# Transposes of u, q and k: from TensorE to the DMA crossbar, with three token-mixing tiles of a batch moved ahead

## The chip, the cores and the metric

One NeuronCore of one Trainium2 chip. The metric is the device time of one execution in microseconds (us); lower is better. A program runs as five instruction streams (TensorE, VectorE, ScalarE, GpSimd, SyncE), in the profile PE, DVE, ACT, POOL and SP, and one set of 16 DMA engines that all streams share. Each stream runs its instructions strictly in the order in which they were written.

## The reference

Two stages follow each other. Shapes: batch 4, 8 heads, 768 tokens, head dimension 64, model width 512, hidden width 2048.

```python
# stage 1: attention with 4 sink tokens and a causal window of 128
scores = scale * np.matmul(q, k.transpose(0, 1, 3, 2))
keep = (pos[None, :] < n_sink) | ((rel >= 0) & (rel < window))    # rel = query - key
a = softmax(np.where(keep, scores, -1e9))
x = np.matmul(a, v)            # then laid out as batch, token, 8*64
# stage 2: a residual MLP block
a1 = alpha1 * x + beta1
tok = np.einsum('ts,bsd->btd', w_tok, a1)        # mixes tokens: each tile needs all of a1
u = x + lam * tok
a2 = alpha2 * u + beta2
out = u + lam * (np.maximum(a2 @ w_ch1, 0.0) @ w_ch2)
```

Inputs and output are fp32; the kernel computes in fp16 with fp32 sums.

## The kernel before, in words

Tokens are cut into six tiles of 128 (`NR`), heads into four pairs (`HP`). For each of the four batches there are two halves.

The attention half of a batch: SP loads q and k for each head pair (`load_qk`, eight loads of 384 KB into the eight `nat` buffers) and v (`load_v`, six loads of 256 KB). `trans` casts one loaded tile to fp16 (`n16`, on POOL), TensorE transposes it in six 128x128 matmuls into a PSUM bank (`tp`, L416), and ACT or DVE copies the result to `qkT` (L226 and L228 are the lines of the copy helper). Then come `sinks`, `scores` (S, L499; exponentials on ACT, L514; masks on DVE, L523), and `pv` (L546), whose normalised result is `x`; POOL makes `xh` = alpha1*lam*x + beta1*lam of it (L588, L591).

The MLP half: `tok` (L677) is six matmuls for each of six token tiles, and needs `xh` of all six. DVE adds the result to x (L686), which gives u, and ACT or POOL casts u to fp16 (`u16`). `uTs` transposes u on TensorE, three token tiles (a "chunk") and two of the four column blocks at a time (`uTp`, L712, six matmuls), and ACT (L723) or DVE (L725) applies alpha2 and beta2 while it copies to `uT`. `mlp1` (L738) has 16 groups of four matmuls for each of the two chunks, each group with a relu on ACT (L744) or DVE (L746) into `hT`. `mlp2` (L762) has four quarters of four matmuls for each token tile; DVE adds its result to x (L773) and SP stores the tile.

The attention of batch b+1 is woven into the MLP of batch b. The order is made by a planner while the kernel is built: `add` records a task with a priority, the engines that may do it and their costs, what it waits for and which buffers it uses; `emit` repeatedly picks the task that can start earliest by its own estimate of time, ties going to the lower priority number, and writes it to that engine's stream. The priorities of the MLP of batch b are `STEP*b` plus the place in the list `seq`; the attention steps of batch b+1 are spread between two places of it, `lo` and `hi`. PSUM has four banks of the kind `d` (used by `tp`, `uTp`, `tok`, `h`, `pv`, `ch`) and two pairs of banks for scores. Loads for batch b+2 wait until the fourth mlp2 tile of batch b is done.

The program that is built has eight completion semaphores for its DMAs, given out in rotation in the order in which the DMAs are written; a DMA that takes one up again first waits, on the engine that issues it, for the DMA that had it before.

Of the kernel before, what the change touches and what calls it, by code (L numbers as in the profile page):

```python
# [39 lines left out]
class Plan:  # L40
# [22 lines left out]
    def emit(self):  # L63
        order = sorted(range(len(self.tasks)), key=lambda i: (self.tasks[i].prio, i))
        rank = {id(self.tasks[i]): r for r, i in enumerate(order)}
        waiting = {id(t): len(t.needs) for t in self.tasks}
        open_ = []

        def admit(t):
            bisect.insort(open_, (rank[id(t)], t), key=lambda x: x[0])  # L70

        for t in self.tasks:
            if not waiting[id(t)]:
                admit(t)
        free = {e: 0.0 for e in (PE, ACT, DVE, POOL, SP)}
        mode = None
        channel = 0.0
        port = 0.0
        done = 0
        while done < len(self.tasks):  # L80
            best = None
            for r, t in open_:
                at = t.ready
                for b in t.uses:
                    if b.t is None and b.home is None:
                        homes = [h for h, x in zip(self.homes[b.kind], self.busy[b.kind]) if not x]
                        n = sum(1 for o in t.uses if o.t is None and o.kind == b.kind)
                        if len(homes) < n:
                            at = None
                            break  # L90
# [12 lines left out]
            open_.remove((r, t))  # L103
            for b in t.uses:
                if b.t is None:
                    spare = [i for i, x in enumerate(self.busy[b.kind]) if not x]
                    b.home = min(spare, key=lambda i: self.homes[b.kind][i])
                    self.busy[b.kind][b.home] = True
                    pool, shape, dtype = self.pools[b.kind]
                    b.t = pool.tile(b.shape or shape, b.dtype or dtype,  # L110
                                    tag=f"{b.kind}_{b.home}", bufs=1, name=b.name)
            until, idle, took = self.fill
            if e == PE and free[PE] < until:
                for _ in range(int((start - max(free[PE], 900.0)) / took)):
# [35 lines left out]
def kernel(  # L150
# [17 lines left out]
    nc = tc.nc  # L168

    B, H, S, D = q.shape  # L170
    P = 128
    DM = H * D
    NR = S // P
# [3 lines left out]
    NC = DM // P  # L177
    NTOK = 384
    D1 = D + 1
    scale = 1.0 / float(D) ** 0.5  # L180
# [40 lines left out]
    add = plan.add  # L221
# [24 lines left out]
    iden = const.tile([P, P], FP16, name="iden")  # L246
# [70 lines left out]
    w1f = const.tile([P, NC, DFF], FP16, name="w1f")  # L317
    w2f = const.tile([P, NF, DM], FP16, name="w2f")

    QK_ORDER = [(hp, t) for hp in range(HP) for t in range(2)]  # L320


# [78 lines left out]
    def trans(p, b, hp, t, engs, evac, cast_p=None, wait=None):  # L401
# [5 lines left out]
        pt = Buf("d", [P, S], FP16, f"tp{b}_{hp}_{t}")  # L407
        o = qkT[b]

        def cast(e):  # L410
# [7 lines left out]
        def ev(e):  # L418
# [282 lines left out]
    def uTs(p, b, chk, cp):  # L701
        if (b, 0) not in uT:
            uT[b, 0] = Buf("uT", None, None, f"uT{b}")
        bo = uT[b, 0]
        pt = Buf("d", [P, 2, NTOK], FP16, f"uTp{b}_{chk}_{cp}")
        us = [u16[b, 3 * chk + i] for i in range(3)]

        def tr(e):
            for ci in range(2):
                c = 2 * cp + ci  # L710
                for i in range(3):
                    nc.tensor.transpose(  # L712
                        pt.t[:, ci, i * P : (i + 1) * P], us[i].t[:, c * P : (c + 1) * P], iden)

        a = add(p, {PE: 330}, tr, [done["u16", b, 3 * chk + i] for i in range(3)], [pt] + us)
        for ci in range(2):
            c = 2 * cp + ci

            def ev(e, ci=ci, c=c):
                o, i = bo.t[:, c, chk * NTOK : (chk + 1) * NTOK], pt.t[:, ci, :]  # L720
                al, be = alpha2_c[:, c : c + 1], beta2_c[:, c : c + 1]
                if e == ACT:
                    nc.scalar.activation(o, i, AF.Identity, bias=be, scale=al)  # L723
                else:
                    nc.vector.tensor_scalar(  # L725
                        out=o, in0=i, scalar1=al, scalar2=be, op0=ALU.mult, op1=ALU.add)

            done["uT", b, chk, c] = add(p + 0.1 + 0.01 * ci, {DVE: 470, ACT: 670}, ev, [a, done["ab2"]], [pt, bo])

    def mlp1(p, b, chk, fi):  # L730
        if fi == 0:
# [110 lines left out]

    STEP = 100.0
    LO = 12
    for b in range(B):
        w0 = STEP * b
        if b == 0:
            seq = [("tok", ti) for ti in range(3)] + [("uT", 0, 0), ("uT", 0, 1)]
            seq += [("tok", ti) for ti in range(3, NR)]
# [4 lines left out]
            m1.insert(3, ("uT", 1, 0))  # L854
            m1.insert(5, ("uT", 1, 1))
        else:
            seq = [("tok", ti) for ti in range(4)]
            seq += [("uT", 0, 0), ("tok", 4), ("uT", 0, 1), ("tok", 5)]
            m1 = [("m1", 0, fi) for fi in range(NF)]
            m1.insert(4, ("uT", 1, 0))  # L860
            m1.insert(6, ("uT", 1, 1))
            m1 += [("m1", 1, fi) for fi in range(NF)]
        seq += m1
        seq += [("m2", ti, part) for ti in range(NR) for part in range(4)]
# [15 lines left out]
            for r in range(NR):  # L880
                load_v(w0 - 10 + r, b + 1, r, late)
        for i, (what, *args) in enumerate(seq):
            {"tok": tok, "uT": uTs, "m1": mlp1, "m2": mlp2}[what](w0 + i, b, *args)
# [61 lines left out]
```

## Time and profile before

| | |
|---|---|
| median of 3 runs | 279.55 us (278.27, 279.55, 552.37) |
| the profiled execution's own time | 278.67 us |
| its span (first to last instruction) | 276.5 us |
| granted TensorE clock | 1.00 |
| busy: PE, DVE, ACT, POOL | 267.9, 143.8, 135.0, 116.6 us |

"Busy" is the time in which at least one instruction of that engine ran. PE's matmuls are pipelined, so a busy PE may still be waiting inside an instruction; what an extra matmul costs is read from the distance between the starts of groups that follow each other. In the chain of waits each piece is the work that released the next one, and the pieces add up to the span.

### The profile page before, as it was taken

The numbers are of one execution on the slowest core, as the hardware profiler recorded it, in microseconds if no ns is written. First come the engines' busy times: TensorE is split into PE (matmuls) and PEld (weight loads), VectorE is DVE, ScalarE is ACT, GpSimd is POOL, SyncE is SP. The second block draws the span as 40 slices with busy tenths as digits, with TensorE's granted clock in tenths as the row PEclk, the third lists the DMA queues.
The fourth block names the chain that finished last, engine by engine and source line by source line (L and its number), as shares of the span: only waits on it lengthen the run. The fifth ranks groups of instructions, "written<-read, shape, count | busy, mean of one in ns | idle before, by whom it ended". The sixth has DMA issues, their size and how long they took to land.

```text
span 276.5 us, 5214 instructions
## 1 busy us (share of the span) xinstructions
PE 267.9 (97%) x2109; PEld 151.8 (55%) x2109; DVE 143.8 (52%) x300; ACT 135.0 (49%) x218; POOL 116.6 (42%) x142
## 2 busy tenths in 40 slices
PE   7999999899899999999999999999999999999994
PEld 7644746555455546756555446655545446565441
DVE  4475745589996446766544147676455144000111
ACT  2688836678731017787640027787720026774000
POOL 5569947725576657203545528103644301000000
PEclk9999999999999999999999999999999999999999
DMA  6999999998001798100011899000002110000221
GB/s 194 335 230 365 366 305 276 255 377 307 4 2 76 241 341 219 40 0 2 0 39 40 250 350 235 5 0 0 2 38 78 40 76 2 0 0 2 76 76 76
DMA packets 42765, 36.77 MB, mean 133 GB/s; under 512 B 26347, under 2 KB 34547, under 8 KB 42742
## 3 DMA queue, kind: packets, MB, share of 16 engines
q1 hardware_dynamic: 42720, 36.45, 41.9%
q8 instruction: 16, 0.26, 0.4%
q14 instruction: 7, 0.06, 0.1%
q10 hardware_dynamic: 22, 0.01, 0.0%
HBM read 30.16 MB, written 6.29 MB: 132 GB/s over the span
## 4 chain that ended last, share of the span: by engine, by line
PE 79%; DMA 13%; DVE 4%; POOL 1%; issue 0%; SPq 0%; DVEq 0%; POOLq 0%
PE ch L762 30%; PE h L738 26%; PE tok L677 8%; DMA nat<-in_q_dram 6%; DMA wst_w<-in_moe_w_ch_dram 5%; PE S L499 3%; PE pv L546 3%; PE tp L416 3%; DMA lb_b<-in_moe_beta_dram 3%; DVE E L523 2%; PE uTp L712 1%; PE pv L539 1%; DVE qkT L228 1%; PE S L494 1%; PE sk L447 1%; PE idle L218 1%
## 5 line engine op out<-in xcount | busy, mean ns | idle before, releaser
L738 PE MATMUL h<-uT,w1f 128*128 128x384 f16 x512 | 91.8, 326 | 1.1 <-ACT qkT L226 0.9
L762 PE MATMUL ch<-w2f,hT 128*128 128x512 f16 x384 | 88.0, 379 | 0.0
L738 PEld LDWEIGHTS <-w1f 128*128 128x128 f16 x512 | 47.4, 98 | 32.0 <-issue 4.1
L762 PEld LDWEIGHTS <-hT 128*128 128x128 f16 x384 | 35.8, 98 | 40.1 <-issue 0.8
L744 ACT ACTIVATE hT<-h 128x384 f16<-128x384 f32 x96 | 46.6, 494 | 21.3 <-PE h L738 19.7
L588 POOL TENSOR_TENSOR tmp<-x,la_b 128x512 f32<-128x512 f32 x18 | 24.5, 1358 | 62.1 <-DVE x L570 62.1
L773 DVE TENSOR_TENSOR x<-x,ch 128x512 f32<-128x512 f32 x24 | 16.5, 687 | 58.7 <-PE ch L762 58.6
L514 ACT ACTIVATE E<-S 128x1024 f16<-128x1024 f32 (+1 forms) x42 | 40.3, 1004 | 8.4 <-PE S L499 4.6
L226 ACT CAST u<-x 128x512 f16<-128x512 f32 x19 | 11.7, 619 | 61.7 <-DVE x L686 61.7
L677 PE MATMUL tok<-xh,wtokT 128*128 128x512 f16 x144 | 34.0, 379 | 0.0
L228 POOL CAST n<-nat 128x768 f16<-128x768 f32 x28 | 22.7, 829 | 17.3 <-PE tp L416 9.2
L746 DVE TENSOR_SCALAR hT<-h 128x384 f16<-128x384 f32 x32 | 17.8, 556 | 17.6 <-PE h L738 16.8
L591 POOL TENSOR_TENSOR xh<-tmp,lb_b 128x512 f16<-128x512 f32 x18 | 25.2, 1399 | 1.4
L686 DVE TENSOR_TENSOR x<-x,tok 128x512 f32<-128x512 f32 x24 | 16.4, 688 | 17.0 <-PE tok L677 12.7
L677 PEld LDWEIGHTS <-wtokT 128*128 128x128 f16 x144 | 13.7, 98 | 14.9
L570 DVE TENSOR_TENSOR x<-pv,rec 128x256 f32<-128x256 f32 x48 | 20.4, 424 | 1.7
L523 DVE TENSOR_TENSOR E<-E,maskn 128x1024 f16<-128x1024 f16 x25 | 20.2, 833 | 0.0
L546 PE MATMUL pv<-vf,E 128*128 128x65 f16 x328 | 18.4, 193 | 1.5 <-DVE E L523 0.9
L546 PEld LDWEIGHTS <-E 128*128 128x128 f16 x328 | 15.6, 98 | 7.6 <-DVE E L523 1.5
L228 DVE COPY qkT<-tp 128x768 f16<-128x768 f16 x16 | 15.2, 952 | 6.2 <-PE tp L416 6.2
L416 PE MATMUL tp<-iden,n 128*128 128x128 f16 x192 | 16.1, 223 | 0.7 <-POOL n L228 0.6
L226 ACT COPY qkT<-tp 128x768 f16<-128x768 f16 x16 | 12.8, 798 | 7.8 <-PE tp L416 7.7
(93 smaller groups left out, 226.2 us busy)
## 6 DMA issues: line engine op xcount, KB each, us to landing
wst_w<-in_moe_w_ch_dram SPq DMA_DIRECT2D x16, 512.0 KB, 5.5
nat<-in_q_dram SPq DMA_DIRECT2D x16, 384.0 KB, 6.0
nat<-in_k_dram SPq DMA_DIRECT2D x16, 384.0 KB, 8.2
out_dram<-x SPq DMA_DIRECT2D x24, 256.0 KB, 2.0
vnat<-in_v_dram SPq DMA_DIRECT2D x18, 256.0 KB, 6.3
wtn<-in_moe_w_tok_dram SPq DMA_DIRECT2D x6, 384.0 KB, 6.0
v<-in_v_dram SPq DMA_DIRECT2D x12, 128.0 KB, 5.4
lam_b<-in_moe_lam_dram SPq DMA_DIRECT2D x1, 256.0 KB, 9.2
```

Of the source, the lines that this page charges most:

```text
L226: nc.scalar.copy(o, i)
L228: engine[e].tensor_copy(o, i)
L416: nc.tensor.transpose(pt.t[:, r * P : (r + 1) * P], n16.t[:, r, :], iden)
L514: nc.scalar.activation(eT.t, pS.t[:, :, 0 : n * w].rearrange("p e (i w) -> p e i w", i=n), AF.Exp, scale=scale)
L523: nc.vector.tensor_mul(ev, ev, m.to_broadcast(list(ev.shape)))
L546: nc.tensor.matmul(po.t[:, hl, :], eT.t[:, e_, off + i, c : c + P], vf[j][:, h, :], start=(r < 2 and n == 0), stop=(n == len(parts) - 1 an ...
L588: nc.gpsimd.tensor_mul(tmp.t, bx.t.rearrange("p h d -> p (h d)"), la1_b)
L591: nc.gpsimd.tensor_add(bh.t, tmp.t, lb1_b)
L677: nc.tensor.matmul(pt.t, wtokT[:, si, ti * P : (ti + 1) * P], hs[si].t, start=(si == 0), stop=(si == NR - 1 and b > 0))
L738: nc.tensor.matmul(ph.t, w1f[:, c, fi * P : (fi + 1) * P], bu.t[:, c, chk * NTOK : (chk + 1) * NTOK], start=(c == 0), stop=(c == NC - 1))
L744: nc.scalar.activation(bh.t[:, fi, :], ph.t, AF.Relu)
L762: nc.tensor.matmul(pc.t, bh.t[:, fi, nt * P : (nt + 1) * P], w2f[:, fi, :], start=(fi == 0), stop=(fi == NF - 1))
```

## The change

`u` of a token tile, from the second chunk of the first batch on, is no longer transposed by TensorE: ACT issues one DMA transpose per token tile (128x512 fp16) from `u16` to `uT`, and DVE then applies alpha2 and beta2 in place, in four operations per chunk. The first chunk of the first batch stays on TensorE (`first_uT`). For batches 2 and 3 (numbered from 0; `XB = 2`) q and k are transposed the same way, one DMA per tensor and head pair (128x768 fp16), and are loaded with tokens in plain order, so that each piece of a load is one row of 64 floats. A DMA transpose of q or k also waits for that of the third u tile of the batch before. The priorities of the first three `tok` tiles of batches 1 to 3 are lowered by `LEAD = 46`, which puts them among the last mlp2 tiles of the batch before, and the attention of the next batch is asked to end six places earlier in the list. The planner gets a model of the queue of transposes.

```diff
@@ Plan.emit
+            elif t.lands:
+                ring = max(ring, free[e] + 1600.0) + t.lands * (2 if channel > free[e] + 1600.0 else 1)
+                channel = max(channel, free[e] + 1600.0) + t.lands
+                t.seen = ring + 300.0
@@ load_qk
-        done["nat", b, hp, t] = add(
-            p, {SP: 480}, lambda e: nc.sync.dma_start(bf.t, src.rearrange("h (p r) d -> p h (r d)", p=P)),
-            [wait], [bf], lands=1110)
+        if b < XB:
+            ...
+        else:
+            src = src.rearrange("h s d -> (h s) d").rearrange("(x p) d -> p x d", p=P)
+            done["nat", b, hp, t] = add(
+                p, {SP: 700}, lambda e: nc.sync.dma_start(
+                    bf.t.rearrange("p e (r d) -> p (e r) d", r=NR), src), [wait], [bf], lands=1740)
@@ trans
-        a = add(p, {PE: 330}, tr, [a, wait], [n16, pt])
+        if b >= XB:
+            done["qkT", b, hp, t] = add(
+                p, {ACT: 1100}, lambda e: nc.scalar.dma_start_transpose(
+                    o.t[:, 2 * hp + t, :].rearrange("p (r i) -> p r i", r=NR),
+                    n16.t.rearrange("p r i -> p (r i)")),
+                [a, done["uTd", b - 1, 2]] + prior, [n16, o], lands=900)
+            return
+        pt = Buf("d", [P, S], FP16, f"tp{b}_{hp}_{t}")
+        a = add(p, {PE: 330}, tr, [a, wait], [n16, pt])
@@ uTs
+        if b == 0 and ti < 3:
+            if ti == 2:
+                first_uT(p)
+            return
+        done["uTd", b, ti] = add(
+            p, {ACT: 800}, lambda e: nc.scalar.dma_start_transpose(
+                bo.t[:, :, ti * P : (ti + 1) * P], bu.t),
+            [done["u16", b, ti]], [bu, bo], lands=600)
+        if ti % 3 < 2:
+            return
+        chk = ti // 3
+        for c in range(NC):
+            def ev(e, c=c):
+                o = bo.t[:, c, chk * NTOK : (chk + 1) * NTOK]
+                nc.vector.tensor_scalar(
+                    out=o, in0=o, scalar1=alpha2_c[:, c : c + 1], scalar2=beta2_c[:, c : c + 1],
+                    op0=ALU.mult, op1=ALU.add)
+            done["uT", b, chk, c] = add(
+                p + 0.1 + 0.01 * c, {DVE: 170}, ev,
+                [done["uTd", b, 3 * chk + i] for i in range(3)] + [done["ab2"]], [bo], port=True)
@@ the list of the MLP half
-            seq = [("tok", ti) for ti in range(4)]
-            seq += [("uT", 0, 0), ("tok", 4), ("uT", 0, 1), ("tok", 5)]
+            seq = [("tok", ti) for ti in range(NR)]
             m1 = [("m1", 0, fi) for fi in range(NF)]
-            m1.insert(4, ("uT", 1, 0))
-            m1.insert(6, ("uT", 1, 1))
             m1 += [("m1", 1, fi) for fi in range(NF)]
 ...
+            if b and what == "tok":
+                p = w0 + i - (LEAD if args[0] < 3 else 0)
+            else:
+                p = w0 + i
+            {"tok": tok, "m1": mlp1, "m2": mlp2}[what](p, b, *args)
+            if what == "tok":
+                uTs(p + 0.3, b, *args)
 ...
-            lo, hi = (1, ns - 8) if b else (LO, ns - 6)
+            lo, hi = (1, ns - 14) if b else (LO, ns - 12)
```

More of the change, by code (lines that the diff above doesn't have):

```diff
@@ L77, in emit @@
         channel = 0.0
+        ring = 0.0
         port = 0.0
@@ L318 @@
     w2f = const.tile([P, NF, DM], FP16, name="w2f")
+    XB = 2
     QK_ORDER = [(hp, t) for hp in range(HP) for t in range(2)]
@@ L331, in load_qk @@
         src = (q, k)[t][b, 2 * hp : 2 * hp + 2]
-        done["nat", b, hp, t] = add(
-            p, {SP: 480}, lambda e: nc.sync.dma_start(bf.t, src.rearrange("h (p r) d -> p h (r d)", p=P)),
-            [wait], [bf], lands=1110)
+        if b < XB:
+            src = src.rearrange("h (p r) d -> p h (r d)", p=P)
+            done["nat", b, hp, t] = add(
+                p, {SP: 480}, lambda e: nc.sync.dma_start(bf.t, src), [wait], [bf], lands=1110)
+        else:
+            src = src.rearrange("h s d -> (h s) d").rearrange("(x p) d -> p x d", p=P)
+            done["nat", b, hp, t] = add(
+                p, {SP: 700}, lambda e: nc.sync.dma_start(
+                    bf.t.rearrange("p e (r d) -> p (e r) d", r=NR), src), [wait], [bf], lands=1740)
     def load_v(p, b, r, wait=None):
@@ L406, in trans @@
         n16 = Buf("n16", None, None, f"n16_{b}_{hp}_{t}")
-        pt = Buf("d", [P, S], FP16, f"tp{b}_{hp}_{t}")
         o = qkT[b]
@@ L699, in tok, with first_uT, tr, ev @@
         done["u16", b, ti] = add(p + 0.2, {ACT: 620, POOL: 640}, uc, [a], [bx, bu])
-    def uTs(p, b, chk, cp):
+    def first_uT(p):
+        bo = uT[0, 0]
+        us = [u16[0, i] for i in range(3)]
+        for cp in range(2):
+            pt = Buf("d", [P, 2, NTOK], FP16, f"uTp0_{cp}")
+            def tr(e, pt=pt, cp=cp):
+                for ci in range(2):
+                    c = 2 * cp + ci
+                    for i in range(3):
+                        nc.tensor.transpose(
+                            pt.t[:, ci, i * P : (i + 1) * P], us[i].t[:, c * P : (c + 1) * P], iden)
+            a = add(p, {PE: 330}, tr, [done["u16", 0, i] for i in range(3)], [pt] + us)
+            for ci in range(2):
+                def ev(e, pt=pt, ci=ci, c=2 * cp + ci):
+                    o, i = bo.t[:, c, 0:NTOK], pt.t[:, ci, :]
+                    al, be = alpha2_c[:, c : c + 1], beta2_c[:, c : c + 1]
+                    if e == ACT:
+                        nc.scalar.activation(o, i, AF.Identity, bias=be, scale=al)
+                    else:
+                        nc.vector.tensor_scalar(
+                            out=o, in0=i, scalar1=al, scalar2=be, op0=ALU.mult, op1=ALU.add)
+                done["uT", 0, 0, 2 * cp + ci] = add(
+                    p + 0.1 + 0.01 * ci, {DVE: 470, ACT: 670}, ev, [a, done["ab2"]], [pt, bo])
@@ L702, in uTs @@
+    def uTs(p, b, ti):
         if (b, 0) not in uT:
             uT[b, 0] = Buf("uT", None, None, f"uT{b}")
[L704 to L728, printed above, removed]
+        bo, bu = uT[b, 0], u16[b, ti]
@@ new lines, in uTs @@
+        if b == 0 and ti < 3:
[12 more added lines that the diff above has]
+                o = bo.t[:, c, chk * NTOK : (chk + 1) * NTOK]
+                nc.vector.tensor_scalar(
+                    out=o, in0=o, scalar1=alpha2_c[:, c : c + 1], scalar2=beta2_c[:, c : c + 1],
[3 more added lines that the diff above has]
+                [done["uTd", b, 3 * chk + i] for i in range(3)] + [done["ab2"]], [bo], port=True)
@@ L844 @@
     LO = 12
+    LEAD = 46.0
     for b in range(B):
@@ L847 @@
         if b == 0:
-            seq = [("tok", ti) for ti in range(3)] + [("uT", 0, 0), ("uT", 0, 1)]
-            seq += [("tok", ti) for ti in range(3, NR)]
+            seq = [("tok", ti) for ti in range(NR)]
             m1 = []
@@ L853 @@
                     m1 += [("m1", chk, fi) for fi in range(4 * qd, 4 * qd + 4)]
-            m1.insert(3, ("uT", 1, 0))
-            m1.insert(5, ("uT", 1, 1))
-        else:
-            seq = [("tok", ti) for ti in range(4)]
-            seq += [("uT", 0, 0), ("tok", 4), ("uT", 0, 1), ("tok", 5)]
+        else:
+            seq = [("tok", ti) for ti in range(NR)]
             m1 = [("m1", 0, fi) for fi in range(NF)]
-            m1.insert(4, ("uT", 1, 0))
-            m1.insert(6, ("uT", 1, 1))
             m1 += [("m1", 1, fi) for fi in range(NF)]
@@ L882 @@
         for i, (what, *args) in enumerate(seq):
-            {"tok": tok, "uT": uTs, "m1": mlp1, "m2": mlp2}[what](w0 + i, b, *args)
+            if b and what == "tok":
+                p = w0 + i - (LEAD if args[0] < 3 else 0)
+            else:
+                p = w0 + i
+            {"tok": tok, "m1": mlp1, "m2": mlp2}[what](p, b, *args)
+            if what == "tok":
+                uTs(p + 0.3, b, *args)
         if b + 1 < B:
             nb = b + 1
-            lo, hi = (1, ns - 8) if b else (LO, ns - 6)
+            lo, hi = (1, ns - 14) if b else (LO, ns - 12)
             steps = [("T", i) for i in range(8)] + [("sk",)]
```

## The prediction

> **What bounds the kernel now.** I read the page's busy row and 40 slices first, then the chain of waits, then the list of who waited for whom, and last the chain and the 2 us windows around the start of batch 1.
>
> ```profile
> PE 267.9 (97%) x2109; PEld 151.8 (55%) x2109; DVE 143.8 (52%) x300; ACT 135.0 (49%) x218; POOL 116.6 (42%) x142
> PE   7999999899899999999999999999999999999994
> DMA  6999999998001798100011899000002110000221
> PE 79%; DMA 13%; DVE 4%; POOL 1%; issue 0%; SPq 0%; DVEq 0%; POOLq 0%
> ```
>
> PE is busy in every slice; no other engine passes 52%. The chain gives PE 79%, and its 13% of DMA lies before 57 us, where weights are still arriving.
>
> ```profile
> 98.78 1.29 PE tok L677 x6
> 100.08 0.86 PE ch L762 x4
> 100.94 3.88 PE tok L677 x18
> 104.83 0.67 PE tp L416 x12
> 105.50 0.34 PE uTp L712 x6
> 105.83 1.30 PE tok L677 x6
> ...
> 113.69 0.34 PE tp L416 x6
> 114.02 0.34 PE uTp L712 x6
> 114.36 0.76 PE h L738 x4
> ```
>
> The pieces follow each other without a hole: six transposes cost PE 0.336 us, a tok tile 1.295, an mlp1 group 0.65, an mlp2 quarter 0.86. The transposes stand between other groups and hide their own latency. All of PE's own waits after 57.5 us are under 2 us together (`pv` for DVE 1.5), so what is taken from PE there shortens the run, and every new wait of PE lengthens it.
>
> ```profile
> POOL n L228 <- DMA nat<-in_k_dram: 0.5, 1, 0.5
> 96.00:98.00 2.00, 2.00 (x11) 0.91 (x10) 0.00 (x0) 0.00 (x0) 1.92 (x3) 1.00 1.01 351
> 106.00:108.00 2.00, 2.00 (x20) 1.26 (x18) 1.64 (x4) 1.60 (x3) 2.00 (x4) 1.00 1.07 264
> 108.00:110.00 2.00, 2.00 (x17) 1.20 (x15) 1.01 (x2) 1.50 (x3) 1.93 (x5) 1.00 0.97 275
> nat<-in_k_dram SPq DMA_DIRECT2D x16, 384.0 KB, 8.2
> out_dram<-x SPq DMA_DIRECT2D x24, 256.0 KB, 2.0
> ```
>
> The last two columns of the windows are the DMA share and GB/s. From 90 to 112 us the loads for batch 2 keep the DMA engines full. With q and k (pieces of 1536 B) they move 351 GB/s, with v (256 B) 264 to 275. This is just when the new transposes of u are to run.
>
> [...] The trace gives TensorE 0.056 us in a row of six (219 to 223 ns for one alone)[...]; it has no crossbar. [...]
>
> **The change part by part.**
>
> *Removed from PE.* tp of batches 2 and 3: 16 groups of six. uTp: 14 of 16 groups. 30 x 0.336 = 10.1 us. Two of the uTp groups (batch 0, second chunk) stood at 46 us, where the chain runs over weight loads, and gain nothing: 28 count, 9.4 us. The copies to qkT and uT (0.80 to 0.95 and 0.47 to 0.67 us each) also go; ACT and DVE are not the bound.
>
> *What ACT gets.* 37 DMA issues: 21 of u, 16 of q and k. From below, an issue costs what SP's plain ones do, 0.44 to 0.50 us. [...] Landing, from below: 2.0 us, what a 256 KB store takes from issue[...].
>
> *The start of batch 1.* In the changed kernel's order all six tok tiles of batch 1 stand behind the last mlp2 quarter of batch 0; nothing runs ahead there. Set the start of the first at 0. PE is ready for mlp1 at 6 x 1.295 = 7.77. Chunk 0 needs the third tile: matmuls end 4.05, DVE adds to 4.8, POOL casts 0.62 more. But POOL has casts of q and k ahead of it, and the fourth of them waited for its load until 1.5 after the start even before; with 256-byte pieces (1.46 instead of 1.12 us a load) later still. I take the cast done at 5.7, landed at 8.25. Then DVE's four in-place operations: the 128x256 fp16 row of that kind takes 0.22, PSUM rows of 384 take 0.47; I take 0.25 each, 1.0. mlp1 starts at 9.4, a hole of 1.6 us.
> Behind the last u transpose (issued at 9.9[...]) ACT holds four of q/k[...], and only then the relu of the sixth group, so 15.8 to 16.3. With four PSUM banks the tenth group wants that bank at 9.4 + 9 x 0.65 = 15.25: 1.05 us. DVE also holds the second chunk's in-place operations, which wait for the sixth transpose (12.5), ahead of the fifth relu: done at 14.1, wanted at 14.6, no loss. Later q/k transposes wait on ACT for casts that POOL makes behind v loads: 0.5. Batch 1: 3.2 us.
>
> *Batch 2.* Three mlp2 quarters stand among the tok tiles, PE is ready at 7.77 + 2.6 = 10.4, chunk 0 at about 9.3: no hole. ACT alternates u and q/k up to 17.4, and the relu behind is wanted at 18.2. I put 0.5 for late loads.
>
> *Batch 3.* One quarter stands between: ready at 8.63, chunk 0 at 9.05 with no loads about: 0.4.
>
> *The first batch* gets three transposes inside the full DMA stretch, 0.37 us each at 351 GB/s, half of it on the weights' path: 0.5.
>
> *Attention moved.* The scores of batch 2 start at the 28th mlp1 group instead of the 14th. Behind them PE still has about 28 us before the next tok tile; ACT needs some 13 and DVE some 22 (eleven masks at 0.83, twelve normalisations at 0.60, adds and relus). They fit; 0.
>
> **Sum.** Profiled execution 278.67 (span 276.5 and 2.2 around it) - 9.4 + 3.2 + 0.5 + 0.4 + 0.5 = 273.9 us, 1.7% under it; the median of the runs shown is 0.3% above that execution.
>
> **The rivals.**
>
> *Everything is covered.* If transposes land as fast as stores (2.0 us), loads do not delay POOL and ACT issues at 0.5, the holes shrink to almost nothing: 278.67 - 10.1 = 268.6 us. For it: the six-tile order leaves 3.9 us of tok behind the third tile everywhere. Against it: DVE, POOL, an issue and a landing with nothing between are already 0.7 + 0.6 + 2.0 + 1.0.
>
> *The ring of transposes is too slow (slower).* ACT's queue carries 14 transposes for each of batches 1 and 2, in order, beside loads that already fill the engines. If each holds it [...]2.5 and 2.9, the first starting at 3.7: chunk 0 lands at 11.2 and mlp1 starts 4.5 late; chunk 1 lands at 18.7 in front of DVE's relus, 2.9 more; the last q/k lands at 41.9, while PE comes to the scores at 32.7, 9.6 more. Batch 1 loses 17, batch 2 by the same sums 1.9 + 3.5 + 7.5 = 12.9, batch 3 0.9: 278.67 - 9.4 + 0.5 + 30.8 = 300.6. It decides from about 2.0 and 2.3 us each, where the losses eat the 9.4 and reach 284.2. For it: the DMA row, the in-order ACT and POOL queues, and that a transpose can sit on ACT waiting for a load that had its semaphore eight DMAs earlier. Against it: the 128 KB need only 0.5 us at the rate of 256-byte pieces.
>
> *The lead does nothing.* At batch 1 this is seen in the order. If it held at all three, batches 2 and 3 would lose 1.6 more each: 277; inside the forecast's range.
>
> **How the numbers follow.** Forecast 273.9 (chance 0.50; its own range 270 to 281, issue at 0.5 to 1.3 us and landing at 2.0 to 3.5 us), all covered 268.6 (0.14), slow ring 300.6 (0.36, from 284 up). About 2% is what a measurement of this kernel can tell from no change. Faster by over 2% means under 273.1: all of the second case and 0.20 of the first, 0.34. Within 2%: the other 0.30. Slower: 0.36. The range runs from 268 to 295: it leaves out some 0.02 below and, of the slow ring, some 0.15 above.
>
> **What would show it.** Right: PE's busy time down by about 10 us; tp with 96 and uTp with 12 matmuls; a hole of PE of 1 to 3 us before the first mlp1 group of batch 1, none at batch 2; ACT's issue 0.8 to 1.3 us; landings under 4 us. Wrong: landings of 5 us or more, PE waiting for a transpose before the scores of batches 2 and 3, ACT standing at an issue for a load, or DVE's in-place operations near 0.5 us.

## The result, and the profile after

The changed kernel takes 290.99 us (median of 4 runs, 289.57 to 293.29); the kernel before, on the same chip, takes 279.62 us. The ratio is 1.043, 95% interval 1.032 to 1.054: slower by 11 us, where 273.9 us was forecast. One of the four runs of before, at 552.37 us, is a slow one and stays out of the ratio. The profiled execution took 292.28 us with a span of 290.5. The page of the changed kernel, in the order in which the page of before was read:

```profile
span 290.5 us, 4946 instructions
PE 265.4 (91%) x1929; PEld 142.7 (49%) x1929; DVE 159.2 (55%) x316; ACT 109.5 (38%) x176; POOL 129.1 (44%) x152
PE   8889996699699999499999998969999998999995
PEclk9999999889779999899999999999999999999999
DMA  6999999966400699997001399999010114000211
PE 68%; DMA 17%; DVE 11%; issue 1%; POOL 1%; ACT 0%; SPq 0%; ACTq 0%; DVEq 0%; POOLq 0%
```

TensorE lost its 180 matmuls (2109 to 1929), but its busy time fell by 2.5 us only (at half the clock a matmul is busy for about twice as long: in two of the windows below, 11 of them fill 3.4 us at half the clock and 20 at the full one), and its row now has slices of 6 and 4, which means that it stands. The clock row has sevens and eights, where before it was nines throughout. DMA (13 to 17%) and VectorE (4 to 11%) have taken eleven points of the chain from TensorE. Who made TensorE wait (engine, line, releaser: total us, times, longest), and two stretches of the chain of waits, the first batch and the start of batch 1:

```profile
PE h L787 <- DVE uT L771: 9.1, 6, 3.8
PE pv L567 <- DVE E L544: 3.0, 4, 2.2
PE h L787 <- ACT hT L793: 1.6, 1, 1.6
```

```profile
43.38 10.92 DMA uT<-u
54.30 0.98 issue
55.28 1.85 DVE uT L771 x4
...
108.75 1.31 PE tok L698 x6
...
110.81 0.63 ACT u L232
...
111.46 5.52 DMA uT<-u
...
117.77 4.77 DMA uT<-u
...
122.55 3.27 DMA vnat<-in_v_dram
125.82 1.75 DVE uT L771 x3
```

Where before six transposes and a tok tile followed each other without a hole, the chain now runs over transposes of u in flight: 10.9 us for one in the first batch, 5.5 and 4.8 us for two in batch 1. After them VectorE's in-place operations wait, and only then can mlp1 start. The rows of the new operations say what each costs (duration in ns, min/median/max), and the three lines under them what landings took, counted from the start of the issue: from 40 to 60 us, from 100 to 130, and from 230 to 255 us. In the last of these stretches no load runs. The trace tells the landing of one of three transposes, of two of six and of three of six:

```profile
L761 ACTq DMA_TRANSPOSE uT<-u x21: 1204/1212/1859, 40.9 to 245.9; - x21
L771 DVE TENSOR_SCALAR uT<-uT,ab x28: 361/374/872, 55.3 to 249.2; 128x384 f16<-128x384 f16 x28
L442 ACTq DMA_TRANSPOSE qkT<-n x16: 1226/1307/1894, 121.5 to 197.8; - x16
...
DMA to landing us min/median/max: 10.9/10.9/10.9
...
DMA to landing us min/median/max: 4.8/5.6/6.5
...
DMA to landing us min/median/max: 2.3/2.4/2.7
```

The same transfer lands in 2.4 us where no load runs and in 5.6 or 10.9 us beside loads. That is the first thing that the prediction did not have. The second is the clock. In these windows (start:end, length, busy us of PE, PEld, DVE, ACT and POOL, granted clock, DMA share, which can pass 1 here, GB/s) holes of TensorE alternate with the stretches behind them:

```profile
53.90:55.70 1.80, 0.00 (x0) 0.10 (x1) 0.42 (x2) 0.49 (x1) 0.22 (x1) 1.00 1.10 246
56.30:59.70 3.40, 3.32 (x11) 1.39 (x11) 1.68 (x4) 0.98 (x2) 0.69 (x1) 0.51 1.02 374
74.50:76.60 2.10, 0.04 (x2) 0.00 (x0) 2.10 (x4) 0.18 (x1) 0.39 (x1) 1.00 0.82 220
76.80:83.60 6.80, 6.16 (x37) 3.22 (x37) 4.53 (x12) 2.62 (x4) 5.02 (x5) 0.50 0.25 77
116.50:120.30 3.80, 0.03 (x1) 0.10 (x1) 1.07 (x3) 0.00 (x0) 1.23 (x2) 1.00 1.31 217
121.20:124.60 3.40, 3.13 (x11) 1.43 (x10) 1.40 (x3) 0.00 (x0) 0.79 (x2) 0.50 0.86 181
180.50:182.20 1.70, 0.02 (x1) 0.10 (x1) 0.39 (x2) 0.00 (x0) 0.26 (x1) 1.00 1.34 214
182.60:186.00 3.40, 3.40 (x20) 1.88 (x20) 3.19 (x7) 0.00 (x0) 1.44 (x2) 1.00 1.30 263
```

After three of the four holes the clock is halved for 3.4 or 6.8 us, 13.6 us in all, which by estimate, from the 11 and 20 matmuls above, costs half of that, 6.8 us. In the clock records of this trace the three stretches last 3.413, 6.827 and 3.413 us and begin at 56.34, 76.82 and 121.19 us, 20.48 and 44.37 us apart, which is 6 and then 13 times 3.413. The first two stand behind holes of 1.8 and 2.1 us.

The length of a hole does not decide alone. In e8 (below) a wait of 2.1 us has no half clock behind it (granted clock 1.00), and in e13 (0.994) there is a stretch of it, 3.4 us, although the longest wait of TensorE from 40 to 105 us is 1.2 us. What goes with the half clock in the trace of the changed kernel is the share of time in which TensorE was busy just before it, in windows of 3.413 us laid end to end so that the three stretches fall on their edges. These are the windows in which the four holes end:

```profile
52.93:56.34 3.41, 1.33 (x8) 0.61 (x7) 1.06 (x3) 1.25 (x3) 1.08 (x3) 1.00 0.83 211
73.41:76.82 3.41, 1.25 (x17) 0.59 (x12) 3.41 (x5) 1.27 (x2) 1.48 (x1) 1.00 0.55 154
117.78:121.19 3.41, 0.82 (x3) 0.38 (x4) 1.27 (x4) 0.00 (x0) 1.11 (x2) 1.00 1.34 232
179.22:182.63 3.41, 1.69 (x9) 0.68 (x7) 1.50 (x4) 0.00 (x0) 0.61 (x1) 1.00 1.36 213
```

TensorE is busy for 39, 37 and 24% of the three that half clock follows, and for 50% of the fourth. From 46.1 to 288.4 us there are 71 such windows, 67 of them at the full clock. The three with half clock behind them are the only ones of the 67 that were busy for under 40%; the other 64, busy for 49% or more, have none behind them. This is read from one trace; no run varied it by itself.

Most of the sum can be found in the trace. TensorE's gaps of more than 0.12 us add up to 21.4 us in the changed kernel and to 4.8 before. These 16.6 us more, with 6.8 us of clock and less the 10.1 us of removed groups, are 13.3 of the 14.0 us by which the span grew; the other 0.7 us is not split. By batch, the end of the last mlp1 group:

| | batch 0 | batch 1 | batch 2 | batch 3 |
|---|---|---|---|---|
| before, us | 74.8 | 136.9 | 198.2 | 252.0 |
| after, us | 84.2 | 146.3 | 210.2 | 266.2 |
| later by | 9.4 | 9.4 | 12.0 | 14.2 |

Most of the loss is in the first batch, which has only three of the 37 new transposes; two of the three stretches at half the clock lie in it, 10.2 us long, and are up to 5.1 of its 9.4 us. Batches 2 and 3 add 4.8 us, though TensorE has less to do there.

### The profile page after: what moved, and what is told of

Same layout as the page of the kernel before. It is cut to its first block, busy times and chain, and to the rows that moved or that the text cites. A ratio compares the mean times of both kernels' runs of the same rounds, so it can differ in the third digit from the quotient of the medians.

```text
span 290.5 us, 4946 instructions
## 1 busy us (share of the span) xinstructions
PE 265.4 (91%) x1929; PEld 142.7 (49%) x1929; DVE 159.2 (55%) x316; ACT 109.5 (38%) x176; POOL 129.1 (44%) x152
## 4 chain that ended last, share of the span: by engine, by line
PE 68%; DMA 17%; DVE 11%; issue 1%; POOL 1%; ACT 0%; SPq 0%; ACTq 0%; DVEq 0%; POOLq 0%
PE ch L811 26%; PE h L787 22%; DMA uT<-u 7%; PE tok L698 7%; DVE E L544 4%; PE S L520 3%; PE pv L567 3%; DMA nat<-in_k_dram 3%; DMA vnat<-in_v_dram 3%; DMA qkT<-n 2%; DMA nat<-in_q_dram 2%; DVE w2f L680 2%; DVE uT L771 1%; PE S L515 1%; DVE x L591 1%
## 5 line engine op out<-in xcount | busy, mean ns | idle before, releaser
L787 PE MATMUL h<-uT,w1f 128*128 128x384 f16 x512 | 94.1, 338 | 11.8 <-DVE uT L771 9.1
L787 PEld LDWEIGHTS <-w1f 128*128 128x128 f16 x512 | 50.5, 101 | 52.6 <-issue 22.0
L793 ACT ACTIVATE hT<-h 128x384 f16<-128x384 f32 x82 | 39.6, 492 | 61.2 <-PE h L787 38.1
L535 ACT ACTIVATE E<-S 128x1024 f16<-128x1024 f32 (+1 forms) x42 | 40.5, 1002 | 22.6 <-PE S L520 11.8
L609 POOL TENSOR_TENSOR tmp<-x,la_b 128x512 f32<-128x512 f32 x18 | 26.0, 1445 | 46.2 <-DVE x L591 42.6
L795 DVE TENSOR_SCALAR hT<-h 128x384 f16<-128x384 f32 x46 | 25.4, 555 | 27.6 <-PE h L787 26.1
L232 ACT CAST u<-x 128x512 f16<-128x512 f32 x11 | 6.8, 618 | 60.5 <-DVE x L707 56.0
L707 DVE TENSOR_TENSOR x<-x,tok 128x512 f32<-128x512 f32 x24 | 16.4, 686 | 21.5 <-PE tok L698 16.6
L544 DVE TENSOR_TENSOR E<-E,maskn 128x1024 f16<-128x1024 f16 x25 | 27.1, 1105 | 1.1 <-ACT E L535 1.0
L234 POOL CAST vf<-vnat 128x512 f16<-128x512 f32 x18 | 11.3, 634 | 20.2 <-DMA vnat<-in_v_dram 18.1
L234 POOL CAST u<-x 128x512 f16<-128x512 f32 x13 | 8.0, 613 | 20.9 <-DVE x L707 16.7
L771 DVE TENSOR_SCALAR uT<-uT,ab 128x384 f16<-128x384 f16 x28 | 11.6, 475 | 8.5 <-DMA uT<-u 8.5
```

The lines of the kernel that those rows point to most:

```text
L234: engine[e].tensor_copy(o, i)
L535: nc.scalar.activation(eT.t, pS.t[:, :, 0 : n * w].rearrange("p e (i w) -> p e i w", i=n), AF.Exp, scale=scale)
L544: nc.vector.tensor_mul(ev, ev, m.to_broadcast(list(ev.shape)))
L609: nc.gpsimd.tensor_mul(tmp.t, bx.t.rearrange("p h d -> p (h d)"), la1_b)
L787: nc.tensor.matmul(ph.t, w1f[:, c, fi * P : (fi + 1) * P], bu.t[:, c, chk * NTOK : (chk + 1) * NTOK], start=(c == 0), stop=(c == NC - 1))
L793: nc.scalar.activation(bh.t[:, fi, :], ph.t, AF.Relu)
```

## The experiments

Ratios are to the kernel before on the same chip, whose medians were 278.7 to 279.6 us; one hundredth of a ratio is 2.8 us. The times are medians of 4 to 20 runs.

| run | what is transposed by the crossbar | us | ratio, 95% interval |
|---|---|---|---|
| e1_b0_pe | u of batches 1 to 3; q/k | 282.51 | 1.010 (1.006 to 1.015) |
| e2_qk_pe | u as in the change; no q/k | 289.46 | 1.035 (1.031 to 1.039) |
| e3_u_pe | no u; q/k | 274.72 | 0.984 (0.980 to 0.988) |
| e4_warm | all, with idle matmuls in three holes | 287.99 | 1.028 (1.023 to 1.034) |
| e5_lead_only | nothing; lead and order kept | 280.64 | 1.005 (1.002 to 1.009) |
| e6_early_loads | as e1, loads earlier | 284.22 | 1.020 (1.015 to 1.025) |
| e7_u_last | u of batch 3; q/k | 272.76 | 0.978 (0.974 to 0.983) |
| e8_qk_no_lead | as e3, no lead | 275.57 | 0.990 (0.987 to 0.993) |
| e9_u23_early | u of batches 2, 3; q/k; last loads earlier | 276.77 | 0.992 (0.989 to 0.994) |
| e10_u23 | as e9, loads as in the change | 276.53 | 0.991 (0.988 to 0.994) |
| e11_qk_last | u and q/k of batch 3 | 277.18 | 0.992 (0.990 to 0.995) |
| e12_front_only | u of batch 0, second chunk; q/k | 285.30 | 1.026 (1.019 to 1.034) |
| e13_front_masks | as e12, w2 products placed as in e3 | 281.08 | 1.010 (1.006 to 1.015) |
| e14_front_extra | as e3, three more transposes that nobody reads | 276.72 | 0.993 (0.990 to 0.995) |
| e15_u23_qk2 | as e11, with u of batch 2 and last loads earlier | 276.01 | 0.987 (0.982 to 0.991) |
| e16_u23_qk_late | as e9, q/k transposes later | 292.01 | 1.044 (1.040 to 1.048) |

"q/k" is q and k of batches 2 and 3, as in the change. The kernels choose by a list of (batch, chunk) what of u goes over the crossbar; what is not in it takes the path of `first_uT`:

```diff
-        if b == 0 and ti < 3:
-            if ti == 2:
-                first_uT(p)
+        if (b, ti // 3) not in UDMA:
+            if ti % 3 == 2:
+                pe_uT(p, b, ti // 3)
             return
```

### Undoing the parts: e1, e2, e3

e1: `UDMA` without (0, 1).

> The second chunk of u of batch 0 goes back to TensorE; all else as changed. Theory F (the front: the three transposes amid the weight loads, 10.9 us to landing, make PE late and the late weights then make VectorE late; with two of the three halvings of the clock): the first tok tile of batch 1 starts near 98 to 99 us instead of 108.6, and the run takes 281 us (279 to 284). Theory Q (the in-order ACT and POOL queues behind transposes and loads in batches 1 and 2 cost the most): the front is only moved about, 287 to 290.

Ratio 1.010 instead of 1.043: the front costs 0.033, 9.2 us. Batch 0's mlp1 ends at 75.1 us as before (74.8), so that the whole lag of that batch is gone. What is left is still slower than before: waits of 2.1 and 4.3 us ahead of mlp1 of batches 1 and 2, with half clock behind the first and from within the second on (3.4 and 6.8 us).

e2: `XB = 4`, all q and k on TensorE with the old loads.

> q and k of batches 2 and 3 go back to TensorE, with their old loads (pieces of 1536 B); u stays on the crossbar everywhere. PE gets 5.4 us of work back. Theory F: the 10 us of the front stay, 287 to 290. Theory Q: without the 16 long transposes and with shorter loads the holes of batches 1 and 2 (4 and 8 us) go, 281 to 284.

289.46 us, ratio 1.035. The slow ring, in which the q/k transposes fill ScalarE's queue, would have had to give back most of the loss. It falls as the main cause.

e3: `UDMA` empty, so that of the transposes only those of q and k are left.

> All transposes of u go back to TensorE; q and k of batches 2 and 3 stay on the crossbar with pieces of 256 B. PE gets 4.7 us back. Theory F: no late front, no hole before mlp1, clock at 1.0 throughout, 277 to 281. Theory Q: holes of 4 to 8 us at the relus behind q/k transposes remain in each of batches 1 and 2, 284 to 288.

274.72 us, faster than before. The u transposes are the loss (0.059 from the changed kernel, 16 us), and the q/k transposes by themselves are a gain. The two don't simply add up. Beside the u transposes those of q and k gain nothing that can be seen: e2 has 16 groups (5.4 us) more on TensorE than the changed kernel and is 0.008 below it, within the intervals. Nor do the u transposes alone cost 16 us: from e5 (below), with no transposes, to e2 it is 0.030, 8.4 us. What they do to each other no run takes apart; both stand in ScalarE's one row.

### The clock: e4

Matmuls that no one reads are put into the first three of the four holes above, in front of the group that waits. For two of them it is a group of mlp1:

```diff
         def mm(e):
+            for _ in range(WARM.get(("h", b, chk, fi), 0)):
+                nc.tensor.matmul(ph.t[:, 0:P], iden, iden, start=True, stop=True)
             for c in range(NC):
```

> As changed, with 22, 26 and 44 idle 128-column matmuls put in front of three groups that PE waits for (second chunk of batch 0, pv of tile 1 of batch 1, first mlp1 group of batch 1); they fit in the holes of 2.1, 2.8 and 4.1 us and shorten the idle stretches to under 1.7 us. If the holes make the clock fall to half (3.4, 6.8 and 3.4 us in the trace, 6.8 us lost), the clock stays at 1.0 and the run takes 284 to 286 us; if the clock falls for another reason, 291 or a little more.

287.99 us: 0.015 less than the changed kernel, 4.1 us, for more work on TensorE; the two intervals just overlap, and 284 to 286 us was expected. The halved stretches behind the second and the third hole are gone. The first stayed, and a new hole of batch 2 was followed by one (windows as above):

```profile
176.80:179.90 3.10, 0.02 (x1) 0.12 (x2) 0.46 (x2) 0.00 (x0) 0.22 (x1) 1.00 1.33 235
180.20:183.60 3.40, 3.40 (x11) 1.57 (x11) 2.20 (x5) 0.00 (x0) 1.39 (x2) 0.50 1.16 222
```

So the clock is a loss of its own behind the waits, of a few microseconds, and not the bulk. The first stretch stayed although its hole was partly filled: a wait of 1.6 us was left ahead of the group.

### Lead and q/k: e5, e8, e11

e5: `UDMA` empty and `XB = 4`, so that no transpose is left; the lead stays, and with it the new places of the attention and of TensorE's transposes of u in the list. e8: e3 with `LEAD = 0.0`. e11: e7 with `XB = 3`.

> Every transpose is TensorE's again, of u and of q and k in all four batches, with the old loads; of the change only the lead of three tok tiles is left. Theory S (the lead itself is worth little, and the 4.7 us that e3_u_pe won over the kernel before come from the q/k transposes leaving TensorE): within 2 us of the kernel before, 278 to 280 us. Rival L (the lead is what wins in e3_u_pe): 275 to 276 us. If the lead costs time of its own: over 281 us.

> As e3_u_pe (u on TensorE, q and k of batches 2 and 3 on the crossbar), with the lead of the tok tiles set to nothing. Theory S (the q/k transposes alone win): 274 to 276 us, as e3_u_pe. Rival L (the lead is what wins, or is needed as cover): 278 to 280 us.

> As e7_u_last, but q and k go over the crossbar in the last batch alone (those of batch 2 on TensorE with the old loads). Theory: each batch of q/k groups that leaves TensorE is worth its 8 x 0.34 = 2.7 us, since the wait for its landing is covered: 2 to 3 us above e7_u_last, 274.5 to 276 us. Rival (the q/k transposes of batch 2, issued beside the loads of the batch after, cost what they remove, and the gain is all of the last batch): 272 to 273.5 us.

The lead with the new order costs 0.005 (1.5 us); the lead by itself, beside the q/k transposes, gains 0.006 (1.6 us, e8 to e3). Both are small, as theory S has it. From e5 to e3, 16 groups of q/k leave TensorE: 0.021, 5.9 us, where 16 x 0.336 is 5.4. e11 puts those of batch 2 back: 0.014 above e7, 3.9 us, a little more than expected. With u on TensorE, in batches 0 to 2 at least, the q/k transposes gain all that they remove. That their landing and their issue are covered, since nobody needs their results at once, is in line with this.

### What makes u slow: e6, e7, e9, e10

e7: `UDMA` for batch 3 alone. e6: e1 with `late = done["h", b - 1, 1, 15]`, so that the loads of the next batch may start earlier. e10: `UDMA` for batches 2 and 3. e9: e10 with that earlier `late` for the loads of the last batch.

> As e1_b0_pe (first batch all on TensorE, u of batches 1 to 3 on the crossbar), but the q, k and v loads of the next batch no longer wait for the fourth pair step of the batch before: they wait for the last mlp1 tile of that batch, so that they start earlier and should be through before the u transposes are issued. Theory C (the u transposes land late, 4.5 to 7 us, because the loads of the next batch share the DMA engines with them): landings fall to 2.5 to 3.5 us, the holes of TensorE ahead of the first mlp1 tiles of batches 1 and 2 (2.1 and 4.4 us in e1_b0_pe) fall under 1.6 us, the clock stays up, and the time is 275 to 278 us. Rival Q (the order of issues on ScalarE's queue makes the holes, whatever the loads do): landings fall or not, holes stay, 281 to 284 us.

> u is transposed by the crossbar in the last batch alone, where no loads of a next batch run (its landings were 2.3 to 2.7 us in the changed kernel), and on TensorE in batches 0 to 2; q and k as in the changed kernel. Theory C (loads beside the transposes are the cost): the last batch's transposes are nearly free, and beside e3_u_pe (274.7 us) TensorE is rid of 8 groups of 0.34 us, 2.7 us, less a hole of about 1.1 us: 273 to 274.5 us. Rival (a u transpose costs by its issue and its wait anywhere): 275 to 277 us.

> As e7_u_last, with the u of batch 2 on the crossbar too, and the loads of the last batch alone started earlier (after the last mlp1 tile of batch 1 instead of after its fourth pair step), so that they are through when the u of batch 2 is issued, as they were in e6_early_loads (landings of 2.4 us there at batch 2). Theory C (loads beside the transposes are the cost): landings at batch 2 of 2.3 to 3 us, no hole over 1.6 us and no fall of the clock there, and 8 groups of 0.34 us less on TensorE: 270 to 272.5 us. Rival (a u transpose costs by its issue and wait anywhere, or the earlier loads only put the collision elsewhere, as in batch 1 of e6_early_loads): 273 to 278 us.

> As e9_u23_early, but with the loads of the last batch where the changed kernel has them. Theory C: the u transposes of batch 2 meet the loads, land after 4.5 to 7 us, TensorE has a hole of 2 to 4.5 us ahead of the first mlp1 tile of batch 2 and a fall of the clock of 3.4 to 6.8 us that costs half its length: 274.5 to 278 us, 3 us or more above e9_u23_early. Rival: the same as e9_u23_early within 1 us.

e7 is the fastest of all, 272.76 us, 2.2% under the kernel before: in a batch with no loads and no q/k transposes the u transposes don't cost, and may gain what they remove (0.006 against e3, 1.7 us, with intervals that overlap). A batch has four groups of u, two for each chunk, so that 1.3 us was to be had; the texts of e7, e9 and e15 count eight, 2.7 us, which is twice too many. Its trace has no hole over 0.8 us after 50 us and no half clock:

```profile
span 271.3 us, 5027 instructions
PE 260.2 (96%) x1989; PEld 143.8 (53%) x1989; DVE 149.9 (55%) x303; ACT 121.2 (45%) x198; POOL 119.0 (44%) x143
PEclk9999999999999999999999999999999999999999
```

e10 and e9 differ by one thing, whether the loads of the last batch run beside the u transposes of batch 2. Landings of u from 155 to 200 us, e10 first, then e9:

```profile
DMA to landing us min/median/max: 6.1/6.5/6.7
```

```profile
DMA to landing us min/median/max: 2.4/2.7/3.0
```

This shows what makes them land late: the loads. Transposes that ScalarE issues take a median of 6.5 us to landing beside the loads that SyncE issues, and 2.7 us without them. Yet the time did not move (276.77 and 276.53), so the landing is not all of it, and half of theory C falls: it said 3 us. In the trace of e10 TensorE waits no more than 0.6 us for the u of batch 2, late as it lands. In e9 the relus are late instead. ScalarE's longest wait and TensorE's two, from 158 to 185 us:

```profile
ACT hT L794 <- DMA qkT<-n: 15.0, 1, 15.0
```

```profile
PE vsp_None L488 <- ACT hT L794: 1.7, 1, 1.7
PE h L788 <- DVE hT L796: 1.6, 1, 1.6
```

From 164.5 to 179.5 us ScalarE issues ten transposes of u and q/k, 1.2 to 2.3 us each, and does nothing else; its relu for the tenth mlp1 group starts at 179.5, 5 us after that group has run (the hole of 1.7 us). The sixth u transpose stands behind three of q/k in that row and goes at 171.6; VectorE's in-place operations of the second chunk wait for it until 175.8, with the relu of the ninth group behind them (the hole of 1.6 us). 3.4 us of half clock follow. e6 has the same twofold picture. In its batch 2 the landings fell to 2.4 us and the hole ahead of mlp1 went, as theory C said; in its batch 1 the loads still ran (6.8 us, hole 4.1), and ScalarE's lateness made a hole of 2.6 us ahead of the sinks of batch 2. It was slower than e1.

### The issues on ScalarE: e15, e16

> As e9_u23_early (276.8 us), but q and k of the last batch go back to TensorE, so that in batch 2 ScalarE's queue carries the six u transposes alone. Theory A (with the landings at 2.7 us, what still costs in batch 2 is ScalarE: 13 issues of 1.25 us in one row from 161 to 179.5 us, the relus of mlp1 behind them): the holes of e9_u23_early ahead of mlp1 groups 10 to 12 of batch 2 (3.2 us, and 1.7 us of halved clock) go, TensorE gets 8 groups of 0.34 us back: 274 to 276 us. Rival (ScalarE is not it): 278 to 280 us.

The edit was `XB = 3`, and this puts q and k of batch 2 back on TensorE, not those of the last batch: their transposes leave batch 1, and batch 2 keeps its row of 14. So the run doesn't test what its text says. It is e11 with the u of batch 2 and the earlier last loads added, and beside e11 it gains 0.006, 1.6 us, about the 1.3 us that the four groups are. ScalarE's unbroken row of issues ends 7.1 us after mlp1 has begun (at 178.2 and 171.1 us), in e9 11.5 us after, and the one hole, 1.0 us, is again a wait for ScalarE's relu. This fits a row of issues that costs little where fewer relus stand behind it.

e16: the q/k transposes wait for the relus of the first chunk:

```diff
-                [a, done["uTd", b - 1, 2]] + prior, [n16, o], lands=900)
+                [a, done["h", b - 1, 0, 15]] + prior, [n16, o], lands=900)
```

> As e9_u23_early, but the q/k transposes of the next batch wait for the last mlp1 group of the first chunk instead of the third u transpose, so that they stand on ScalarE after the relus of that chunk. Theory A (ScalarE's row of issues ahead of the relus is what costs): the holes ahead of mlp1 groups 10 to 12 of batch 2 go and the time falls by 2 to 5 us, to 272 to 275 us, unless the scores then wait for the last q/k. Rival (ScalarE is not it, or the block of issues only stands ahead of other relus): 276 to 279 us.

292.01 us, what its text had as an exception: the scores then wait for the last q/k. Behind them tok tiles wait too, 6.2 us in all for `xh`, and 13.7 us run at half the clock. TensorE's wait before the sinks, and the chain from 120 to 140 us:

```profile
PE sk L469 <- ACT ks L232: 3.8, 1, 3.8
```

```profile
122.13 7.45 DMA qkT<-n x2
...
130.59 7.10 DMA qkT<-n
137.85 0.20 ACT ks L232
```

So the row of issues can't simply be moved back either. It stands ahead of relus where it is, or ahead of the scores. That ScalarE's row is the rest of batch 2's loss rests on the trace of e9 and is supported by the holes of e15; no run took it away alone.

### The front: e12, e13, e14

e12: `UDMA = [(0, 1)]`. e13: as e12, with w2's products on the engines of e3:

```diff
-                p, {DVE: 700, POOL: 1270},
+                p, {POOL: 1270} if a in (8, 9, 12) else {DVE: 700},
```

e14: e3, and besides

```diff
+            if b == 0 and ti >= 3:
+                sp = Buf("spare", None, None, f"spare{ti}") if ti < 5 else Buf("tmp", [P, NC, P], FP16, "spare5")
+                add(p, {ACT: 800}, lambda e: nc.scalar.dma_start_transpose(sp.t, bu.t),
+                    [done["u16", b, ti]], [bu, sp], lands=600)
```

> As e3_u_pe with one thing added: the second chunk of u of the first batch, three transposes, goes over the crossbar, as in the changed kernel. Theory F (these three, issued while the weights are being loaded, cost the changed kernel the 8.5 us by which e1_b0_pe is faster): landings of 9 to 11 us, and 7 to 10 us above e3_u_pe (274.7 us), 282 to 285 us. Rival (the loss needs the later u transposes too, which then come late and meet the loads): under 278 us.

> As e12_front_only (285.3 us), with the 16 products of w2 by lam put on the engines that they have in e3_u_pe (13 on VectorE, 3 on GpSimd); the planner had put 8 on each in e12_front_only, where pairs of them ran at 1.7 us on both engines at once. Theory M (that shift of engines frees the weight buffers late, so that the last weight load is issued at 74.4 us instead of 65.6, and makes most of the loss): the last weight load is issued before 70 us and the time is 279 to 282 us. Rival W (the loss is the wait for landings of 11 us, and what is late after it): 284 to 286 us.

> As e3_u_pe, with u all on TensorE, and with the three crossbar transposes of the second chunk of u of the first batch issued besides, into spare buffers that nothing reads: their traffic, their issues on ScalarE and their hold on the u16 buffers are there, but TensorE waits for none of them. Rival W (the wait for the landing is the loss): within 2 us of e3_u_pe (274.7 us). Theory T (what they take from the loads of the weights, and from ScalarE, is the loss): 279 to 284 us. In between, the two share it as the number says.

Three transposes added to e3 cost 0.042, 11.8 us, against 9.2 us when they are taken from the changed kernel. e13 and e14 divide it. The rows of the weights, from 30 to 90 us (ns, first and last start), in e3 and then in e12:

```profile
L391 SPq DMA_DIRECT2D wst_w<-in_moe_w_ch_dram x14: 368/390/4990, 41.3 to 65.6; - x14
L681 DVE TENSOR_TENSOR w2f<-wst_w,lam_b x13: 678/684/1758, 59.6 to 80.9; 128x512 f16<-128x512 f32 x13
...
L681 POOL TENSOR_TENSOR w2f<-wst_w,lam_b x3: 1540/1709/1711, 65.2 to 72.8; 128x512 f16<-128x512 f32 x3
```

```profile
L391 SPq DMA_DIRECT2D wst_w<-in_moe_w_ch_dram x14: 367/388/3509, 40.6 to 74.4; - x14
...
L681 POOL TENSOR_TENSOR w2f<-wst_w,lam_b x8: 1255/1398/1796, 60.9 to 79.3; 128x512 f16<-128x512 f32 x8
L681 DVE TENSOR_TENSOR w2f<-wst_w,lam_b x8: 684/1050/1758, 68.6 to 87.8; 128x512 f16<-128x512 f32 x8
```

The planner, which counts the in-place operations on VectorE, gave GpSimd five more products of w2, at 1.26 us or more instead of 0.68; in the changed kernel they are split 8 and 8 as well. Where both engines do one at the same time each takes longer: in the trace of the changed kernel, from 71.5 to 75.4 us, VectorE's take 1.75 us and GpSimd's 1.71, where the shortest are 0.68 and 1.26. The four staging buffers come free late, and the last weight load is issued at 74.4 us instead of 65.6. With the products put back (e13) it is issued at 71.0. The differences between the four runs:

- the planner's shift of products: 0.016, 4.5 us (e12 to e13);
- traffic, issues and buffers of the three transposes, with nobody waiting: 0.008, 2.3 us (e3 to e14);
- what remains, 0.018, 5.0 us (e14 to e13): TensorE's second chunk now depends on the landings, which were 10.5 us in e13 and 11.4 in e14.

The first is good to some 2 us, the others to some 1.5 us, and the planner splits the products in e14 once more differently, 11 and 5. They hold the clock too: 6.8 us at half the clock in e12, 3.4 in e13, none in e14. That the third is the wait itself is not shown. In the trace of e13 TensorE waits 1.0 us for the in-place operations of that chunk; what else it lost there is half clock (up to 1.7 us) and other waits for VectorE (`tp` 1.4, `pv` 1.0 us).

## Why the prediction was wrong

Its direction was wrong, and its range, up to 295, held the time only because of its slow rival. Step by step:

**Removed from TensorE, 9.4 us: right by itself.** The 16 q/k groups gave 5.9 us (e5 to e3) where u stays on TensorE. In the changed kernel itself they gave nothing that can be seen (e2): that the sum prices q/k and u as if the two didn't meet was wrong.

**The first batch, 0.5 us: the step that failed.** It measured 9 to 12 us. The step priced the three transposes by their bytes (0.37 us each at 351 GB/s). It left out that the second chunk's mlp1 waits for the landing with little to hide it (2.1 us in the trace), that a transpose in the midst of the weight loads landed after 10.9 us, that the planner answers a new DVE task by moving others (4.5 us, e12 to e13), and the half clock, which follows twice in this batch (up to 5.1 us). These pieces overlap.

**A landing, from 5.7 to 8.25 in the sum: right alone, wrong beside loads.** The figure was the author's estimate; no trace before the change showed it. Measured, a landing is 2.4 us where no load runs, and 5.6 and 5.5 us (medians of two in batch 1 and four in batch 2, 4.5 to 7.1) beside loads. The sum took it as if the transposes had the engines to themselves, although the page of before showed the DMA full at just that time (a share of 1.01 from 96 to 98 us).

**ScalarE's issue.** What the sum took for u and for q/k was the author's estimate; no trace before the change showed it. Measured were 1.21 us for u (128x512, median of 21) and 1.31 us for q/k (128x768, median of 16): 1.5 times the elements, 1.08 times the time.

**VectorE in place, 0.25 us each:** 0.37, up to 0.87 beside GpSimd. But mlp1 starts after the first of the four, so that the 1.0 us of the sum was too much.

**Start of batch 1, hole 1.6 us:** 3.85 us. The third tile's cast was done 5.4 us after the first tok tile's start (5.7 in the sum), its transpose landed at 11.2 (8.25), mlp1 started at 11.6 (9.4). The landing is the whole of the error. That nothing ran ahead there was right, so that the lead does nothing at batch 1; over all it gains some 1.6 us (e8 to e3).

**Start of batch 2, no hole; batch 3, 0.4 us:** 1.7 and 1.1 us.

**The relus behind ScalarE's row, 1.05 us:** one hole of 1.6 us, in batch 2 instead of batch 1, and one of 0.9 us for GpSimd's cast of v behind its load. The mechanism was in the text and the size near; that the second chunk's in-place operations cost nothing fell with the landings (e9).

**Half clock after a hole:** not in the text, so put at nothing. About 6.8 us of the changed kernel; e4, which filled holes, got 4.1 us back.

**The rivals.** The slow ring had the sign and the two means, full engines and ScalarE's in-order row (in e9 a relu waits 15.0 us behind transposes in it). But it named q/k, late before the scores, as its largest term, and batch 0 as 0.5. e3 shows that the q/k transposes gain by themselves; beside those of u (e2) they gain nothing, but cost far less than the rival had. "The lead does nothing" is nearly so.

Open is what the u of batch 1 costs alone. By difference (e1 less e3, with batch 2's and batch 3's shares from e10 and e7) it would be 5.4 us: 7.2 - 3.5 + 1.7.

## What to carry to other kernels

Price a transfer that the bounding engine waits for by what is queued on the DMA engines at its moment, not by its own bytes alone: the same 128x512 transpose landed here after 2.4 us without loads and after 5.5 and 10.9 us beside them. Look at the DMA row of the slice in which it will run, and use it where other work lies between landing and use, or where no loads run: here that was q/k, and u in the one batch without loads, which together give the fastest version (e7, 272.76 us; the interval of e3, with q/k alone, overlaps its own). A matmul pipeline that runs without holes can pay twice for a new one, by the hole and by the clock behind it: here holes of 1.8 and 2.1 us had 3.4 and 6.8 us at half the clock behind them. And where a planner places the work, a new task on one engine also moves old tasks to others, so that the order of all engines is to be compared before a part is priced at nothing.

## What was not expected of the hardware

- Holes of TensorE of 1.8 and 2.1 us were followed by 3.4 and 6.8 us at half the clock; one of 1.7 was not, nor a wait of 2.1 in e8, while e13 has 3.4 us of half clock with no wait over 1.2 us from 40 to 105 us. In the changed kernel the stretches start 6 and 13 times 3.413 us apart, each behind a window of 3.413 us in which TensorE was busy for 24 to 39% of the time.
- A DMA transpose holds ScalarE for 1.21 us (median) when it moves 128x512 fp16, and for 1.31 us when it moves 128x768.
- A 128x512 transpose lands after 2.4 us where no load runs, 5.5 us beside loads of q, k and v, and 10.9 us beside those of the weights.
